# Products with carried state in a retention block: from 128x64 array tiles to eight 64x32 tiles with an exchange of heads in PSUM

## Chip, cores, metric

One core of one Trainium2 chip. The metric is the device time of one execution in microseconds (us), as a median over runs. The kernel before took 1078.23 us (median of 3 runs, 1076.21 to 1079.26).

## The reference

A retention block (a linear attention with a decay per head) feeds an MLP with PReLU; everything is fp32. Cut to what matters:

```python
B, H, S, D = 8, 8, 576, 64
scores = q @ k^T / sqrt(D)                       # per batch and head
Dmat   = gamma[h] ** (i - j) where i >= j else 0
ret    = (scores * Dmat) @ v
x = ret.transpose(0, 2, 1, 3).reshape(B * S, H * D)        # 4608 x 512
h = x @ w_in                                     # 512 -> 2048
out = (max(h, 0) + alpha * min(h, 0)) @ w_out    # 2048 -> 512
```

## The kernel before

TensorE works the matmuls and adds up their results in PSUM, a memory in banks, from which ScalarE and VectorE copy them. Retention is worked in chunks of 64 tokens, nine for a sequence, for two heads at a time: 32 pairs of heads, which the code calls n. Inside a chunk it is scores times v (the "values"). What comes from earlier chunks is q times a carried sum of k^T v (the "products with the sums", one for each of the chunks 1 to 8). Between these small blocks stand units of the MLP, which fill TensorE: 28 records of `ph` and 14 of `po` a unit (a record is one MATMUL entry of the profile).

```python
def half(x):                       # 64 of the 128 partitions
    return slice(x * C, (x + 1) * C)

def states(n, kn, vn):             # k^T v of each chunk, then the carried sums
    ... 32 records of 64x64 matmuls into ps[0], ps[1] ...
    su = attn.tile([P, NJ - 1, D], FP32, tag="su", name=f"su_{n}")   # head h2 in half h2
    ... ScalarE and VectorE form the carried sums in su ...
    for h2 in range(2):            # sm: a 128x128 block diagonal of both heads, zero elsewhere
        nc.scalar.copy(sm[half(h2), :, h2], su[half(h2)])

def values(n, vn, qT, at):
    b, c = pairs[n]
    pv = [ps_tile(n, p2, [P, NM, C], f"pv{p2}_{n}") for p2 in range(2)]   # even, odd chunks
    for m in range(NM):
        for p2 in range(2 if 2 * m + 1 < NJ else 1):
            for h2 in range(2):
                nc.tensor.matmul(pv[p2][half(h2), m], vn[half(p2), m, h2],
                                 at[h2][half(p2), m], start=(m == 0), stop=False, ...)
    for j in range(1, NJ):         # the products with the sums
        for h2 in range(2):
            nc.tensor.matmul(pv[j % 2][half(h2), j // 2], sm[:, j - 1, h2],
                             qT[:, chunk(j)], start=False, stop=(j >= NJ - 2), ...)
    for p2 in range(2):
        put_x(b, c, p2, pv[p2])    # ScalarE copies pv into the MLP's input
```

The product for one head contracts 128 rows, of which 64 are zeros: it uses one half of the array's columns and all its rows, so two such products fit at a time, and half of what they multiply is nothing.

## Time and profile before

| | before |
|---|---|
| median | 1078.23 us |
| span of the profiled run | 1076.6 us |
| TensorE busy | 1054.3 us (98%) |
| a block of products with the sums, from its first start to the next block | 1.082 us, 32 records |
| from the products of pair 8 to the end | 864.08 us |

The prediction below shows the lines and how to read them. One note: the start of this kernel, up to about 200 us, varies from run to run; the last row of the table leaves it out and is the sharper measure. I take it from the timeline, from the start of the first product of pair 8 (212.55 us) to the end of the span:

```profile
212.55 1.15 PE L565 MATMUL pv<-qT,sums 128*64 128x64 f32 x32
```

### The profile page before, as it was taken

Reading aid. Unit: us, or ns where it says so; the run is one execution under the profiler, and the core shown is the slowest. Engines: PE = TensorE matmul, PEld = TensorE weight load, DVE = VectorE, ACT = ScalarE, POOL = GpSimd, SP = SyncE. Lnnn points to the kernel's source line nnn. Section 1 sums busy time; section 2 is a strip of 40 time slices with the busy share of each in tenths; the row PEclk is TensorE's granted clock in tenths of the full one; section 3 lists DMA queues with packets and bytes.
Section 4 is the critical chain, followed back from the end, with each engine's and each line's share of the span. In section 5 each row is a group of like instructions: output and inputs, shape, how many; then the busy total and the mean of one; then the engine's idle time right before and its main releaser. Section 6 shows DMA issues by size and latency. Waiting matters only on the chain.

```text
span 1076.6 us, 25072 instructions
## 1 busy us (share of the span) xinstructions
PE 1054.3 (98%) x10321; PEld 927.9 (86%) x10321; DVE 747.0 (69%) x1958; ACT 191.1 (18%) x549; POOL 217.4 (20%) x260
## 2 busy tenths in 40 slices
PE   6899999999999999999999999999999999999998
PEld 5666666899999999999999999999999999999997
DVE  5688612678687777786777777786768676667575
ACT  3666422211110111110100111111111110000000
POOL 4368743411020102010102110201011000100000
PEclk9989999999999999999999999999999999999999
DMA  8857413212222222211112222122222100000000
GB/s 199 242 155 231 100 25 63 76 36 64 45 65 43 56 46 52 47 43 34 35 43 40 60 46 65 35 65 46 65 46 54 24 21 1 21 1 21 1 21 20
DMA packets 212050, 63.25 MB, mean 59 GB/s; under 512 B 201168, under 2 KB 201184, under 8 KB 211936
## 3 DMA queue, kind: packets, MB, share of 16 engines
q1 hardware_dynamic: 209504, 61.04, 24.2%
q8 instruction: 82, 1.34, 0.5%
q10 hardware_dynamic: 2432, 0.60, 0.3%
q14 instruction: 32, 0.26, 0.1%
HBM read 52.17 MB, written 9.44 MB: 57 GB/s over the span
## 4 chain that ended last, share of the span: by engine, by line
PE 93%; DVE 2%; DMA 2%; ACT 1%; issue 1%; POOL 0%; SPq 0%; ACTq 0%; DVEq 0%
PE ph L392 38%; PE po L314 36%; PE ph L350 5%; PE po L329 4%; PE pv L565 3%; PE pv L560 2%; PE ps L523 2%; PE pu L538 2%; PE pt L494 1%; DMA raw<-in_moe_w_in_dram 1%; DMA w_in<-in_moe_w_in_dram 1%; DVE wc L245 1%; DVE wc L248 0%; DMA a<-in_moe_alpha_dram 0%; DMA kn<-in_k_dram 0%
## 5 line engine op out<-in xcount | busy, mean ns | idle before, releaser
L314 PE MATMUL po<-w_out,g 128*128 128x256 f32 x1792 | 407.8, 379 | 0.0
L314 PEld LDWEIGHTS po<-w_out,g 128*128 128x128 f32 x1792 | 330.8, 190 | 39.7
L403 DVE TENSOR_TENSOR g<-ph,g 128x256 f32<-128x256 f32 (+1 forms) x512 | 187.4, 387 | 180.2 <-PE ph L392 103.6
L392 PE MATMUL ph<-xb,w_in 128*128 128x128 f32 x2048 | 277.7, 279 | 0.0
L392 PEld LDWEIGHTS ph<-xb,w_in 128*128 128x128 f32 x2048 | 253.1, 192 | 8.2 <-issue 0.5
L392 PE MATMUL ph<-xt,w_in 128*128 128x128 f32 x1536 | 213.3, 275 | 0.0
L392 PEld LDWEIGHTS ph<-xt,w_in 128*128 128x128 f32 x1536 | 192.1, 192 | 0.0
L414 DVE TENSOR_TENSOR g<-g 128x128 f32<-128x128 f32 x512 | 144.0, 322 | 7.8
L398 ACT COPY g<-ph 128x128 f32<-128x128 f32 x128 | 34.0, 265 | 479.5 <-PE ph L392 472.0
L462 POOL TENSOR_TENSOR vn<-vn,th 128x512 f32<-128x512 f32 (+1 forms) x60 | 42.0, 718 | 380.9 <-DMA vn<-in_v_dram 380.8
L408 DVE SCALAR_TENSOR_TENSOR g<-g 128x512 f32<-128x512 f32 x128 | 94.3, 737 | 3.9
L406 DVE TENSOR_SCALAR g<-g,alpha 128x256 f32<-128x256 f32 x256 | 88.7, 388 | 4.5
L350 PE MATMUL ph<-xb,w_in 128*128 128x256 f32 x256 | 65.3, 404 | 2.8 <-DVE g L359 2.3
L375 POOL TENSOR_TENSOR xt<-xb,xt 128x256 f32<-128x256 f32 x32 | 25.1, 786 | 175.2 <-ACT xb L451 174.6
L350 PEld LDWEIGHTS ph<-xb,w_in 128*128 128x128 f32 x256 | 48.9, 198 | 13.2 <-issue 4.7
L329 PE MATMUL po<-w_out,g 128*128 128x512 f32 x128 | 57.8, 593 | 1.1 <-DVE g L359 1.1
L451 ACT COPY xb<-pv 128x128 f32<-128x128 f32 (+1 forms) x176 | 29.6, 269 | 129.1 <-PE pv L565 129.1
L329 PEld LDWEIGHTS po<-w_out,g 128*128 128x128 f32 x128 | 24.2, 190 | 24.5 <-issue 22.0
L552 ACT COPY sums<-su 64x512 f32<-64x512 f32 x64 | 39.5, 617 | 29.4 <-DVE su L549 28.6
L527 DVE SCALAR_TENSOR_TENSOR at<-ps,th,mask 128x320 f32<-128x320 f32 x64 | 32.4, 544 | 15.9 <-PE ps L523 15.9
L506 DVE STREAM_TRANSPOSE qT<-qn 128x576 f32<-128x576 f32 x24 | 18.7, 778 | 33.8 <-PE pv L565 30.5
L565 PE MATMUL pv<-qT,sums 128*64 128x64 f32 x1024 | 41.2, 235 | 0.2 <-ACT sums L552 0.2
(90 smaller groups left out, 686.8 us busy)
## 6 DMA issues: line engine op xcount, KB each, us to landing
out_dram<-osb SPq DMA_DIRECT2D x36, 256.0 KB, 2.3
kn<-in_k_dram SPq DMA_DIRECT2D x60, 128.0 KB, 2.9
vn<-in_v_dram SPq DMA_DIRECT2D x60, 128.0 KB, 2.7
kx<-in_k_dram SPq DMA_DIRECT2D x96, 72.0 KB, 2.4
qn<-in_q_dram SPq DMA_DIRECT2D x96, 72.0 KB, 2.5
raw<-in_moe_w_in_dram SPq DMA_DIRECT2D x11, 512.0 KB, 4.3
raw<-in_moe_w_out_dram SPq DMA_DIRECT2D x11, 512.0 KB, 4.6
w_in<-in_moe_w_in_dram SPq DMA_DIRECT2D x5, 512.0 KB, 6.0
```

Source lines behind the costliest of these rows:

```text
L314: nc.tensor.matmul(acc[kb][n // 2][:, n % 2, :], g[:, x, :], w_out[i][:, y, :], start=(i == 0 and n % 2 == 0), stop=(i == NU - 1 and (n % ...
L329: nc.tensor.matmul(acc[kb][m], g[:, 2 * x + m], w_out[i][:, 2 * x:2 * x + 2].rearrange("p x f -> p (x f)"), start=(i == 0 and x == 0), sto ...
L350: nc.tensor.matmul(ph[:, x], w_in[i // UST][:, cc // 2 * 2 + x, cc % 2, f0:f0 + P], xb[kb][:, cc], start=(cc == 0), stop=(cc == NCC - 1))
L392: nc.tensor.matmul(ph[m][:, o], w_in[i // UST][:, l, cc, f0:f0 + P], r[:, cc], start=(n in (0, 3) and cc == 0), stop=(n in (2, 6) and cc = ...
L398: nc.scalar.copy(g[:, 7], ph[0][:, 2])
L403: nc.vector.tensor_tensor(out=o, in0=x0, in1=x1, op=ALU.add)
L406: nc.vector.tensor_scalar(g[:, 4 + 2 * m:6 + 2 * m], g[:, 2 * m:2 * m + 2], 0.0, alpha[:, fc:fc + 1], ALU.min, ALU.mult)
L408: nc.vector.scalar_tensor_tensor(out=g[:, 0:4].rearrange("p x t -> p (x t)"), in0=g[:, 0:4].rearrange("p x t -> p (x t)"), scalar=0.0, in1 ...
L414: nc.vector.tensor_tensor(out=g[:, o, :], in0=g[:, x0, :], in1=g[:, x1, :], op=op)
L462: nc.gpsimd.tensor_tensor(out=t[0:rows, m], in0=t[0:rows, m], in1=th[0:rows, x, None, 2 * c:2 * c + 2, None].to_broadcast([rows, n, 2, D]) ...
L552: nc.scalar.copy(sm[half(h2), :, h2], su[half(h2)])
L565: nc.tensor.matmul(pv[j % 2][half(h2), j // 2], sm[:, j - 1, h2], qT[:, chunk(j)], start=False, stop=(j >= NJ - 2), skip_group_check=True)
```

## The change

Its intent: give each product the 64 rows it needs. A weight tile of 64 rows by 32 columns lets eight matmuls stand in the array (the prediction names the page). Without more, head h2 would always use the rows of half h2 and the columns of half h2, four of the eight tiles. So the odd chunks have their heads exchanged in PSUM (head 0 in partitions 64 to 127), which uses the other four, and the copy out of PSUM puts them back. The block diagonal `sm`, its memset and its two ScalarE copies per pair go away.

```diff
-    sm = const.tile([P, NJ - 1, 2, D], FP32, name="sums")
-    nc.gpsimd.memset(sm, 0.0)
...
             n = min(nm - m, (w - o + 1) // 2)
-            nc.scalar.copy(xb[kb][:, c].rearrange(...)[:, o:o + 2 * n - 1:2], pv[:, m:m + n])
+            to = xb[kb][:, c].rearrange("p (j w) -> p j w", w=C)[:, o:o + 2 * n - 1:2]
+            for h2 in range(2) if par else ():
+                nc.scalar.copy(to[half(h2)], pv[half(1 - h2), m:m + n])
+            if not par:
+                nc.scalar.copy(to, pv[:, m:m + n])
...
-        for h2 in range(2):
-            nc.scalar.copy(sm[half(h2), :, h2], su[half(h2)])
+        return su                                   # su now has bufs=2
...
-                    nc.tensor.matmul(pv[p2][half(h2), m], vn[half(p2), m, h2],
+                    nc.tensor.matmul(pv[p2][half(h2 ^ p2), m], vn[half(p2), m, h2],
...
         for j in range(1, NJ):
             for h2 in range(2):
-                nc.tensor.matmul(pv[j % 2][half(h2), j // 2], sm[:, j - 1, h2],
-                                 qT[:, chunk(j)], start=False, stop=(j >= NJ - 2), ...)
+                for e in range(0, D, 32):
+                    to = (h2 ^ (j % 2)) * D + e
+                    nc.tensor.matmul(pv[j % 2][to:to + 32, j // 2],
+                                     su[half(h2), j - 1, e:e + 32], qT[half(h2), chunk(j)],
+                                     start=False, stop=(j >= NJ - 2), ...)
```

More of the change, by code (lines that the diff above doesn't have):

```diff
@@ L450, in put_x @@
             n = min(nm - m, (w - o + 1) // 2)
-            nc.scalar.copy(xb[kb][:, c].rearrange("p (j w) -> p j w", w=C)[:, o:o + 2 * n - 1:2],
-                           pv[:, m:m + n])
+            to = xb[kb][:, c].rearrange("p (j w) -> p j w", w=C)[:, o:o + 2 * n - 1:2]
[3 more added lines that the diff above has]
+                nc.scalar.copy(to, pv[:, m:m + n])
             m += n
@@ L540, in states @@
                                      skip_group_check=True)
-        su = attn.tile([P, NJ - 1, D], FP32, tag="su", name=f"su_{n}")
+        su = attn.tile([P, NJ - 1, D], FP32, tag="su", bufs=2, name=f"su_{n}")
         g1, g2 = gch[:, 0, c:c + 1], gch[:, 1, c:c + 1]
@@ L550, in states, with values @@
                                        in1=ps[0][:, 1:], op0=ALU.mult, op1=ALU.add)
-        for h2 in range(2):
-            nc.scalar.copy(sm[half(h2), :, h2], su[half(h2)])
-    def values(n, vn, qT, at):
+        return su
+    def values(n, vn, qT, at, su):
         b, c = pairs[n]
@@ L564, in values @@
             for h2 in range(2):
-                nc.tensor.matmul(pv[j % 2][half(h2), j // 2], sm[:, j - 1, h2],
-                                 qT[:, chunk(j)], start=False, stop=(j >= NJ - 2),
-                                 skip_group_check=True)
+                for e in range(0, D, 32):
+                    to = (h2 ^ (j % 2)) * D + e
+                    nc.tensor.matmul(pv[j % 2][to:to + 32, j // 2],
+                                     su[half(h2), j - 1, e:e + 32], qT[half(h2), chunk(j)],
+                                     start=False, stop=(j >= NJ - 2), skip_group_check=True)
         for p2 in range(2):
@@ L595 @@
         load_weights(parts[2])
-        states(n, kn, vn)
+        su = states(n, kn, vn)
         pop_units(cuts[1])
@@ L600 @@
             turned[n + 1] = transposes(n + 1)
-        values(n, vn, qT, at)
+        values(n, vn, qT, at, su)
         del loaded[n]
```

## The prediction

> **What bounds the kernel now.** I read the page's busy rows first, then the table of windows by stage, then the timeline of TensorE around the products that the change touches.
>
> ```profile
> PE 1054.3 (98%) x10321; PEld 927.9 (86%) x10321; DVE 747.0 (69%) x1958; ACT 191.1 (18%) x549; POOL 217.4 (20%) x260
> ```
>
> TensorE is busy for 98% of the span; the next engine, VectorE, for 69%. A share over the whole span can hide stages, so next the windows (columns: stretch, length, then busy time and count of PE, PEld, DVE, ACT, POOL, then granted clock, DMA share, GB/s):
>
> ```profile
> 0.00:60.00 60.00, 45.59 (x619) 36.97 (x620) 38.30 (x97) 32.22 (x77) 28.02 (x42) 0.92 0.87 224
> 60.00:192.00 132.00, 128.53 (x1000) 85.63 (x998) 70.18 (x128) 57.13 (x124) 83.75 (x90) 0.98 0.41 107
> 192.00:915.00 723.00, 723.00 (x7641) 658.00 (x7640) 533.53 (x1430) 92.75 (x316) 97.68 (x119) 1.00 0.22 46
> ```
>
> From 192 to 915 us TensorE has no gap at all: 723.00 of 723.00. The last of the 32 head pairs is worked at 914 us, so there whatever shortens a block of matmuls shortens the kernel by as much, and what leaves ScalarE or GpSimd there is worth nothing. From 60 to 192 us TensorE is idle for only 3.5 us. Only the first 60 us are something else: TensorE has 14 us of idle time, and DMA runs at 87%.
>
> The groups concerned, from the page (busy us, mean ns | idle before, releaser):
>
> ```profile
> L552 ACT COPY sums<-su 64x512 f32<-64x512 f32 x64 | 39.5, 617 | 29.4 <-DVE su L549 28.6
> L565 PE MATMUL pv<-qT,sums 128*64 128x64 f32 x1024 | 41.2, 235 | 0.2 <-ACT sums L552 0.2
> ```
>
> L565 is the product with the carried sums: 16 matmuls per pair, 512 in all, and each fp32 matmul is two records, hence 1024. In all its life it waited 0.2 us for the copies of L552. The mean of 235 ns is a latency, since matmuls overlap, so I take the cost of a block from starts: from its first record to the first record of the next block. Timeline of TensorE in steady state (start us, us, what):
>
> ```profile
> 444.87 0.80 PE L560 MATMUL pv<-at,vn 64*64 64x64 f32 x36
> 445.60 1.15 PE L565 MATMUL pv<-qT,sums 128*64 128x64 f32 x32
> 446.68 1.16 PE L392 MATMUL ph<-xb,w_in 128*128 128x128 f32 x8
> ...
> 459.18 0.81 PE L523 MATMUL ps<-qT,kT 64*64 64x64 f32 x40
> 459.92 1.16 PE L392 MATMUL ph<-xb,w_in 128*128 128x128 f32 x8
> ```
>
> and in another pair:
>
> ```profile
> 906.38 0.69 PE L538 MATMUL pu<-vn,kn 64*64 64x64 f32 x32
> 907.00 1.16 PE L392 MATMUL ph<-xb,w_in 128*128 128x128 f32 x8
> ```
>
> L565 takes 445.60 to 446.68 = 1.08 us for 32 records. L538 does 32 records of the same 64 moving columns in 0.62 us. The difference is the tiling: 128x64 puts two tiles in the array, 64x64 puts four.
>
> **A model from these rows.** Call one record on every tile a round. L538 is 32/4 = 8 rounds in 0.62 us, L523 40/4 = 10 rounds in 0.74, L565 32/2 = 16 rounds in 1.08. From 8 and 16 rounds: (1.08 - 0.62)/8 = 0.0575 us per round, and 0.62 - 8 x 0.0575 = 0.16 us fixed per block. Check: 10 rounds give 0.735, measured 0.74. So a round costs 58 ns with two tiles or four, and a block costs its rounds.
>
> Whether eight fit in a round depends on how fast tiles can be started. Records of L523 that overlap the stretch from 459.00 to the time given, which counts starts (same columns, PE only):
>
> ```profile
> 459.00:459.28 0.28, 0.10 (x4) 1.00 0.00 0
> 459.00:459.29 0.29, 0.11 (x5) 1.00 0.00 0
> 459.00:459.30 0.30, 0.12 (x7) 1.00 0.00 0
> 459.00:459.31 0.31, 0.13 (x8) 1.00 0.00 0
> 459.00:459.34 0.34, 0.16 (x8) 1.00 0.00 0
> 459.00:459.37 0.37, 0.19 (x12) 1.00 0.00 0
> ```
>
> Four starts fall between 459.28 and 459.31: about 7 ns apart, then nothing until the round is over. Eight starts need 8 x 7 = 56 ns, just inside 58. That is the whole margin.
>
> **What the Trainium skill says.** (1) "TensorEngine Tiling (Array Packing)", Available Configurations: 64 rows by 32 columns is 8 tiles; Key Properties: changing the mode drains TensorE. The 0.16 us per block fits that, and the change keeps the number of mode switches in steady state. (2) "TensorE: Matmul & The Clock Gate", Wait - 56ns, not 53.3ns?: starts never come closer than about 25 ns. For tiled matmuls this trace disagrees: 40 in 0.74 us is 18.5 ns each with the fixed part in. (3) The same page, Measured speedup vs the span model: each further tile costs about 4 ns; here I see about 7. (4) "PSUM — Partial Sum Buffer", PSUM bank collisions raise a hardware error: two row tiles must not write one bank and 32-partition quadrant together. With the exchange of heads, odd chunks go to one bank and even ones to the other with the halves swapped, so a quadrant gets one row half in each bank; nothing here shows yet that this runs at full pace.
>
> **The change part by part.**
>
> Matmuls of L565: 16 per pair become 32 (16 x 2 halves of 32 columns), 64 records, on eight tiles: 64/8 = 8 rounds. In the order of the built program, pairs 4 to 31 issue them as four on the odd chunk and four on the even one, eight different tiles in turn. Model: 0.16 + 8 x 0.0575 = 0.62 us, plus four more starts in the last round, 4 x 7 ns = 0.03: 0.65 us. Saved 1.08 - 0.65 = 0.43 us a pair; for the 28 pairs of 4 to 31, all on the TensorE-bound stretch, 28 x 0.43 = **12.0 us**.
>
> Copies of L552: 64 x 617 ns = 39.5 us leave ScalarE (18% busy). Worth nothing after 60 us. The 128x1024 memset of the sums (0.95 us on GpSimd at 1.5 us) goes too; GpSimd then waits for inputs until 6 us, so nothing.
>
> Exchange of heads: the copies of odd chunks into xb become twice as many at half the partitions. 176 copies at about 270 ns now, so some 80 more: +20 us on ScalarE, half of what it gets back. The block before is followed by a 6.3 us unit of the MLP, so the copies stay hidden.
>
> Pairs 0 to 3: the blocks of L565 there run slower (1.9 us, at a clock of 0.92 and mixed with other work), and are 10.4% of the chain of the first 75 us. The order of the built program is poor in two of them: pair 2 issues all even chunks, then all odd ones, so four tiles at a time and no gain; pair 0 is cut by other blocks, some five more mode switches at 0.16 to 0.3 us. Pairs 1 and 3 may save 0.9 us each, and a 0.6 us sums copy at 46 us leaves the chain. I put this at a gain of 1 us, give or take 3.
>
> Sum: 12.0 + 1 = 13. 1078.2 - 13 = **1065.2 us**, 1.2% less.
>
> **The rivals.** (a) Starts bind: a stream of 16 loads and matmuls per 58 ns, twice what L523 needs, may not be fed. At 10 ns a start the block is 64 x 10 + 160 = 0.80 us, saving 0.28 x 28 = 8: about 1070. At 13 ns a start it is 0.99 and the time some 1075. Against it: the 7 ns seen inside a round. For it: that was four in a row, never eight. (b) The two row halves take turns at a bank, since for the first time both write one bank at once (the tiling page warns that different row tiles cannot): four tiles at a time, 16 rounds, 1.08 us, and the time stays at 1077 to 1079. Against it: disjoint quadrants. (c) The 25 ns floor of the skill holds for 32-column tiles: 64 x 25 + 160 = 1.76 us, +0.68 x 28 = 19 us more, 1097. The 18.5 ns above speaks against it. (d) VectorE becomes the bound: it is 74% busy in the steady stretch (533.53 of 723), and 1.5% less span does not fill it. (e) The removed waits on ScalarE free the start more than I think: the first 60 us hold 14 us of idle TensorE, but DMA at 87% is the more likely limit; at most 5 us, 1060.
>
> **Range and chances.** I give the full eight tiles about 70%, a feed limit (a) 20%, (b) 6%, (c) 3%. With the start's give or take 3 us: 1060 to 1073. Faster by over 2% means below 1056.7, or 21.5 us; all of L565 from pair 4 on is 28 x 1.08 = 30 us, so the block would have to fall to 0.35 us or the start give much: 4%. Slower by over 2% needs (c): 3%.
>
> **What would show it.** Right: in steady state the block that replaces L565 has 64 records and 0.62 to 0.70 us from its first start to the next block; windows still show TensorE without a gap from about 192 us; 28 pairs account for about 12 us. Wrong: a block of 0.8 us and more with starts evenly 10 ns or more apart (a); rounds of four (b); a gap before the next block, or a stretch from 192 us on with TensorE idle, waiting for xb; or a start that moves by more than 3 us.

## The result, and the profile after

The changed kernel took 1071.45 us (median of 4 runs, 1071.20 to 1071.68) against 1077.85 for the kernel before (4 runs): 6.4 us less. The ratio of the two is 0.9941, with a 95% interval of 0.9924 to 0.9958. Ratios here are the mean time of one kernel's fast runs over that of the other's fast runs of the same rounds, so not quite the ratio of the medians quoted.

The page of the changed kernel, and its windows by stage (columns as before):

```profile
PE 1048.6 (98%) x11345; PEld 919.7 (86%) x11345; DVE 750.2 (70%) x1958; ACT 178.1 (17%) x565; POOL 216.4 (20%) x259
```

```profile
192.00:915.00 723.00, 723.00 (x8483) 656.95 (x8474) 541.89 (x1437) 84.25 (x335) 103.22 (x125) 1.00 0.22 47
```

TensorE still has no gap in the long stretch. Nothing took the place of the removed work there: whatever the change gained in a block, it kept. The timeline of the block, beside which the prediction's lines at 445.60 and 446.68 are to be read:

```profile
443.65 0.86 PE L567 MATMUL pv<-qT,su 64*32 64x64 f32 x64
444.43 1.16 PE L387 MATMUL ph<-xb,w_in 128*128 128x128 f32 x8
```

The block has 64 records and takes 0.788 us from first start to next block, to within 1 ns in all 28 pairs from 4 to 31; the printed starts, rounded, give 0.78. It was 1.082, and I had predicted 0.65. So each pair saves 0.294 us, not 0.43. Why is to be seen in the counts of the block's records that overlap the stretch from 443 to the time given:

```profile
443.00:443.69 0.69, 0.04 (x7) 1.00 0.00 0
443.00:443.72 0.72, 0.07 (x8) 1.00 0.00 0
443.00:443.89 0.89, 0.24 (x32) 1.00 0.00 0
443.00:443.96 0.96, 0.31 (x33) 1.00 0.00 0
443.00:444.15 1.15, 0.50 (x51) 1.00 0.00 0
443.00:444.30 1.30, 0.65 (x64) 1.00 0.00 0
```

Up to the 32nd record all goes as predicted: eight starts in under 50 ns, then a wait for the round to end, and four rounds, 32 records, in 0.24 us. Then one single start in 70 ns, and the other 31 records take until 444.29. The starts themselves show it more finely: rounds at 0, 80, 136 and 192 ns after the first start, the 32nd record at 239 ns, the 33rd at 267, the 34th at 323, and from 331 ns on a step every 16.8 ns, in which two records start, or only one (at first and at the end). From 331 to 642 ns, the last start, that is 10.7 ns a record.

The same measure as in the table above:

```profile
212.95 0.86 PE L567 MATMUL pv<-qT,su 64*32 64x64 f32 x64
```

From the products of pair 8 (212.95 us) to the end (1069.96) are 857.01 us, against 864.08. The difference of 7.07 is 24 x 0.294. The rest of the result lies in the start, where the changed kernel reached the products of pair 8 0.40 us *later*, though pairs 4 to 7 had saved 4 x 0.294 = 1.18 us. Where that went is in the chain of work that ended last (start, length, what). Before:

```profile
98.26 5.99 DMA w_in<-in_moe_w_in_dram
...
107.58 5.38 PE ph L350 x16
```

and after:

```profile
97.79 6.83 DMA w_in<-in_moe_w_in_dram
...
107.92 6.31 PE ph L345 x16
```

A piece of w_in lands at 104.25 us before and at 104.62 after; ScalarE and VectorE then work off a chain, and only then may TensorE go on. In this run the piece took longer, TensorE waited 3.5 us in place of 2.3, and its 16 records after the wait took 6.31 us in place of 5.38, with the granted clock lower (0.72 in the windows from 104 to 116.3 us, against 0.86 before). So in this pair of profiles, what was gained before 104 us was lost to a DMA's landing and to the lower clock. The clock is of this one profile: in the other two of the changed kernel (e7, e11), and in both of the kernel before, the 16 records took 5.38 us. The longer wait is not: it is 3.2 to 4.4 us in all three profiles of the changed kernel, 1.9 and 2.3 in the two of the kernel before (before, e9).

### The profile page after: what moved, and what is told of

The parts are those of the page before. It is cut to its first block, busy times and chain, and to the rows that moved or that the text cites. A ratio compares the mean times of both kernels' runs of the same rounds, so it can differ in the third digit from the quotient of the medians.

```text
span 1070.0 us, 27161 instructions
## 1 busy us (share of the span) xinstructions
PE 1048.6 (98%) x11345; PEld 919.7 (86%) x11345; DVE 750.2 (70%) x1958; ACT 178.1 (17%) x565; POOL 216.4 (20%) x259
## 4 chain that ended last, share of the span: by engine, by line
PE 94%; DVE 2%; DMA 1%; issue 1%; ACT 1%; SPq 0%; POOL 0%; ACTq 0%; DVEq 0%; POOLq 0%
PE ph L387 39%; PE po L309 36%; PE ph L345 5%; PE po L324 4%; PE pv L567 3%; PE pv L560 3%; PE ps L521 2%; PE pu L536 2%; PE pt L492 1%; DMA w_in<-in_moe_w_in_dram 1%; DVE wc L240 0%; DVE wc L243 0%; DMA raw<-in_moe_w_in_dram 0%; DMA a<-in_moe_alpha_dram 0%; DVE w_in L245 0%
## 5 line engine op out<-in xcount | busy, mean ns | idle before, releaser
L401 DVE TENSOR_SCALAR g<-g,alpha 128x256 f32<-128x256 f32 x256 | 93.3, 406 | 4.5
L448 ACT COPY xb<-pv 64x128 f32<-64x128 f32 (+1 forms) x160 | 38.1, 238 | 158.9 <-PE pv L567 157.0
L370 POOL TENSOR_TENSOR xt<-xb,xt 128x256 f32<-128x256 f32 x32 | 25.2, 788 | 171.8 <-ACT xb L450 171.2
L354 DVE SCALAR_TENSOR_TENSOR g<-g,nalpha,ph 128x256 f32<-128x256 f32 x32 | 13.9, 477 | 39.8 <-ACT ph L350 39.8
L541 ACT COPY su<-pu 128x256 f32<-128x256 f32 x32 | 11.9, 371 | 135.3 <-PE pu L536 135.3
```

Source lines behind the costliest of these rows:

```text
L401: nc.vector.tensor_scalar(g[:, 4 + 2 * m:6 + 2 * m], g[:, 2 * m:2 * m + 2], 0.0, alpha[:, fc:fc + 1], ALU.min, ALU.mult)
L448: nc.scalar.copy(to[half(h2)], pv[half(1 - h2), m:m + n])
```

## The experiments

Two theories of the block of 0.79 us. **Feed and queue**: the first 32 records (64 instructions, a load and a matmul each) stand ready and start at 7 ns each; those behind them are delivered more slowly, whatever the array could take. **Eight tiles**: eight tiles of 32 columns do not overlap fully, because both row halves write one PSUM bank at once or for another reason in the array, which costs each round some 20 ns ((0.788 - 0.16)/8 = 0.078 us in place of 0.058).

### e1: the change without the exchange of heads

```diff
-                    to = (h2 ^ (j % 2)) * D + e
+                    to = h2 * D + e
```

and `half(h2)` for the values, whole copies in put_x.

> The change without the exchange of heads: 64 rows by 32 columns as in the changed kernel, but odd chunks keep their heads in place, so that only four of the eight tiles are used; the sums copies stay away, and the odd chunks need no split copies. Theory F (feed: the block of 0.79 us comes from the rate at which TensorE's sequencer delivers instructions once those waiting in its queue are used up, about 8.4 ns for a load and a matmul): four tiles need a record only every 14.5 ns, so rounds of 58 ns rule again and the block of 64 records takes 0.16 + 16 x 0.0575 = 1.08 us, as before the change. The copies taken off ScalarE are then shown to be worth nothing: 1075 to 1079 us. Rival B (eight tiles do not overlap fully in the array or at PSUM, because both row halves write one bank): row halves write disjoint partitions of a bank here too, so the rounds would be about 78 ns and the block 1.4 us, and the time 1087 us.

```profile
407.86 1.10 PE L567 MATMUL pv<-qT,su 64*32 64x64 f32 x64
408.88 1.16 PE L387 MATMUL ph<-xb,w_in 128*128 128x128 f32 x8
```

The block took 1.028 us, near the 1.08 of the feed theory and far from 1.4. The same 64 records on the same kind of tile run with no pause: starts come in fours, after a first round of 80 ns every 56 ns to the end. So 16 rounds of 56 ns with 32-column tiles, a little less than the 58 ns with 64 columns. The time was 1077.23 us (4 runs, 1074.16 to 1081.05), ratio 1.0014 (0.998 to 1.0048): as before the change. From the products of pair 8 to the end it took 862.76 us, 1.32 less than before, and 24 x (1.082 - 1.028) = 1.30. So the sums copies that left ScalarE (39.5 us of its busy time) are worth nothing on that stretch, as predicted. Of the change's 7.07 us there, 1.32 come with the 64x32 form even when only four of its tiles are used, and the other 5.75 with the use of all eight.

### e2: twice the columns on the eight tiles (wrong result)

```diff
+                    m, x = min(j // 2, NM - 2), min(j, NJ - 2) * C
-                    nc.tensor.matmul(pv[j % 2][to:to + 32, j // 2],
-                                     su[half(h2), j - 1, e:e + 32], qT[half(h2), chunk(j)],
+                    nc.tensor.matmul(pv[j % 2][to:to + 32, m:m + 2],
+                                     su[half(h2), j - 1, e:e + 32], qT[half(h2), x:x + 2 * C],
```

> The changed kernel with each of its 32 products moving 128 columns instead of 64 (wrong result on purpose): the same count of instructions on the same eight tiles, twice the columns. A round of 128 columns is 111.5 ns (28 records of the MLP product in 3.12 us), so a record is needed only every 14 ns. F: the feed keeps up, and the block takes 0.16 + 8 x 0.1115 + 0.03 = 1.08 us, 0.29 more than with 64 columns instead of 0.43 more. B, with a loss that grows with the columns (78 ns in place of 58): 0.16 + 8 x 0.150 + 0.03 = 1.39 us; with a fixed loss of 20 ns in each round: 1.24 us.

```profile
408.69 1.16 PE L568 MATMUL pv<-qT,su 64*32 64x128 f32 x64
409.77 1.16 PE L387 MATMUL ph<-xb,w_in 128*128 128x128 f32 x8
```

The block took 1.086 us, against 1.08 for the feed and 1.24 or 1.39 for the eight tiles. Twice the work on the same tiles costs only 0.30 us more, because the rounds are now long enough for the feed. The starts show the slower feed here too: the first eight fall within 46 ns, but those from the 41st to the 48th take 98 ns, and the round still lasts 109 ns, as the rounds ahead of it do:

```profile
408.00:409.25 1.25, 0.56 (x40) 1.00 0.00 0
408.00:409.36 1.36, 0.68 (x48) 1.00 0.00 0
```

Both row halves write one bank all the time here, so this also removes the bank as a cause.

### e3: the products issued twice (wrong result)

```diff
-        for j in range(1, NJ):
+        for j in [*range(1, NJ), *range(1, NJ)]:
```

> The changed kernel with its 32 products issued twice in a row (wrong result on purpose): 128 records in one block in place of 64. F: the second 64 records all come at the rate of the feed, 8.4 ns each: 0.79 + 0.54 = 1.33 us. If the loss were a single pause behind the first 32 records, and 58 ns for eight tiles after that: 0.79 + 8 x 0.058 = 1.25 us. B, 78 ns in each round: 0.79 + 8 x 0.078 = 1.42 us; a pause that comes again behind every 32 records: about 1.43 us.

Most blocks took 1.415 us. Five from pair 4 on took 1.8 to 3.7; in the longest, TensorE stood still for 2 us inside the block, and the profile shows nothing that it waited for ("issue"):

```profile
583.69 1.45 PE L567 MATMUL pv<-qT,su 64*32 64x64 f32 x124
587.18 0.30 PE L567 MATMUL pv<-qT,su 64*32 64x64 f32 x4 [2.04 <-issue]
```

That fits a feed that runs dry, but what held it up is not shown. I had put the feed theory at 1.33, with 8.4 ns for each record after the 32nd; that missed. The count of starts says what is right (the first start is at 424.40):

```profile
424.00:424.66 0.66, 0.26 (x32) 1.00 0.00 0
424.00:424.98 0.98, 0.58 (x59) 1.00 0.00 0
424.00:425.31 1.31, 0.91 (x94) 1.00 0.00 0
424.00:425.64 1.64, 1.24 (x126) 1.00 0.05 15
```

After the first 32 records in 0.24 us, some 32 come in each 0.33 us: 10.3 ns a record. Within such a stretch two records come every 16.8 ns (8.4 a record), with a slower passage about every 32 records: the last case of the expectation, 1.43 us. The figure 1.42 of the other theory fits as well here, but e1, e2 and e8 exclude it.

### e8: half of the products (wrong result)

```diff
-        for j in range(1, NJ):
+        for j in (1, 2, 7, 8):
```

> The changed kernel with half of its products (chunks 1, 2, 7 and 8 alone; wrong result on purpose): 32 records in the block on the eight tiles, as many as start without a loss in the changed kernel. Q (the loss comes only behind the 32nd record): four full rounds of 56 ns and no pause, 0.24 us to the last start and 0.15 to the next block: 0.39 us. Rival (each round of eight tiles loses 20 ns): 0.16 + 4 x 0.0785 + 0.03 = 0.50 us. The stretch from pair 8's product to the end: 857.0 - 24 x 0.40 = 847.4 us for Q, 850.1 for the rival.

```profile
403.64 0.45 PE L567 MATMUL pv<-qT,su 64*32 64x64 f32 x32
404.02 1.16 PE L387 MATMUL ph<-xb,w_in 128*128 128x128 f32 x8
```

The block took 0.384 us (0.39 expected of the feed and queue, 0.50 of the other), and the stretch from pair 8's product to the end 847.32 us (847.4 expected). So a block of 32 records on eight tiles is free of loss, and the whole loss of the changed kernel's block, 0.788 - 2 x 0.384 + 0.15 (one fixed part counted twice) = 0.17 us, stands behind its 32nd record.

### e5: the same cover of the array with half the records

With the exchange of heads, 64x64 tiles would cover the array too: four tiles, 32 records. But then the values and the products have the same tiling, and different row halves would write the same partitions of a bank with nothing to order them. A small copy out of `pv` on ScalarE, which the products must wait for, orders them. The MLP units of a pair are now dealt to four places instead of three.

```diff
+        if n >= 8 and between:
+            seen = attn.tile([P, 2], FP32, tag="seen", name=f"seen_{n}")
+            for p2 in range(2):
+                nc.scalar.copy(seen[:, p2:p2 + 1], pv[p2][:, 0, 0:1])
+            pop_units(between)                      # an MLP unit
+        w = D if n >= 8 and between else 32
...
-                for e in range(0, D, 32):
+                for e in range(0, D, w):
```

> From pair 8 on the products take 64 rows and 64 columns, with the exchange of heads: 32 records on four tiles, which cover the array as the eight do, with half the instructions. A unit of the MLP stands between values and products (with a small copy out of PSUM on ScalarE that orders the two), since both blocks now have the same tiling and different row halves would write the same partitions of a bank. F: the block takes what the states block takes for 32 records on four tiles, 0.62 us; saved against the changed kernel 24 x (0.79 - 0.62) = 4 us: about 1067.5 us. B (row halves sharing a bank cost the time): the block stays at 0.79 us, and the time at 1071 to 1072 us.

```profile
814.59 0.80 PE L560 MATMUL pv<-at,vn 64*64 64x64 f32 x36
815.31 1.16 PE L387 MATMUL ph<-xb,w_in 128*128 128x128 f32 x8
...
821.66 0.69 PE L573 MATMUL pv<-qT,su 64*64 64x64 f32 x32
822.28 1.16 PE L387 MATMUL ph<-xb,w_in 128*128 128x128 f32 x8
```

The block took 0.625 us, as the feed theory had it. The time did not follow: 1071.7 us (6 runs) where about 1067.5 was expected, ratio 0.9944 (0.992 to 0.9968), and the stretch from pair 8's product to the end took 857.65 us where 857.01 - 24 x 0.163 = 853.1 was due. TensorE had no gap. The missing 4.55 us, 0.19 a pair, are the price of one more visit to small tiles, which is paid in the neighbours. The timeline of the kernel before, between the lines at 446.68 and 459.18 that the prediction shows, has it:

```profile
449.91 3.19 PE L314 MATMUL po<-w_out,g 128*128 128x256 f32 x14
452.94 1.05 PE L392 MATMUL ph<-xb,w_in 128*128 128x128 f32 x8
456.06 3.19 PE L314 MATMUL po<-w_out,g 128*128 128x256 f32 x14
```

The first product of a unit takes 449.91 - 446.68 = 3.23 us behind a small block, and 456.06 - 452.94 = 3.12 behind another unit. The second takes 452.94 - 449.91 = 3.03 ahead of a unit, and 459.18 - 456.06 = 3.12 ahead of a small block. Together 0.20 us, over and above the 0.16 us inside the small block. The unit that e5 puts between its two small blocks shows the same: 821.66 - 815.31 = 6.35 us, against 3.12 + 3.03 = 6.15 for one between units.

### e6: the four-tile products in two halves of 32 moving columns

```diff
+                    for x in (0, 32) if w == D else ():
+                        nc.tensor.matmul(pv[j % 2][to:to + w, j // 2, x:x + 32],
+                                         su[half(h2), j - 1, e:e + w],
+                                         qT[half(h2), j * C + x:j * C + x + 32], ...)
```

> The four-tile form with an MLP unit between values and products, but from pair 8 on each product is issued in two halves of 32 moving columns: again 64 records in the block, on four tiles of 64 columns. Theory Q (feed and queue: 32 records, each a load and a matmul, start at 7 ns, and those behind them come with pauses at about 10 ns): the block is slower than its columns need, about 0.75 to 0.85 us, like the eight-tile block. Rival (the loss belongs to eight tiles of 32 columns): rounds of some 29 ns for four tiles, 16 of them: 0.16 + 16 x 0.029 + 0.02 = 0.64 us. The kernel's time should be 1070 to 1076 us.

The block took 1.126 us, more than either had said, and the one run 1081.94 us: a failed experiment for its question. Four records still came in each 58 ns although they moved half the columns, so something other than the moving columns sets the round. The Trainium skill, "TensorE: Matmul & The Clock Gate", LDWEIGHTS, puts the ns of a load at its columns over 1.2, which gives an estimate of 53 ns for 64 columns and would fit; no run here takes it apart. With rounds that long, the feed was not what bound.

### e4: the changed form from pair 4 on only

Pairs 0 to 3 keep the block diagonal, its copies and the order of before.

```diff
+                if n < 4:
+                    nc.tensor.matmul(pv[j % 2][half(h2), j // 2], sm[:, j - 1, h2], qT[:, chunk(j)], ...)
-                for e in range(0, D, 32):
+                for e in range(0, D, 32) if n >= 4 else ():
```

> The changed form from pair 4 on only; pairs 0 to 3 are worked as before the change, in the order of before, with its sums copies. If the changed order of the start is what costs the changed kernel some 1.6 us there (28 pairs at 0.294 us are 8.2, its span fell by 6.6), this kernel runs at about 1069.8 us. If the start only varies by chance (a DMA's landing and TensorE's clock), it runs at the changed kernel's time, 1071.5 us within 1, and its stretch from pair 8's product to the end is the changed kernel's 857 us.

1069.73 us (6 runs, 1067.23 to 1072.50), ratio 0.9945 (0.9921 to 0.997). By itself this is the figure that had been expected if the changed order of the start costs 1.6 us; but it has to be held against the changed kernel on the same chip, which is e7.

### e7, e9 and e11: the two kernels again

No edit.

> The changed kernel once more, for its time beside the others on this chip and for how much its start varies. Steady stretch from pair 8's product to the end: 857 us again, within 0.2. Time of pair 8's product: somewhere between 209 and 214 us; if the start varies by chance it moves by over 1 us against the first profile's 212.95.

> The kernel before once more, for its profile alone: the stretch from pair 8's product to the end should be 864.1 us again within 0.2, and the time of pair 8's product should move by over 1 us against 212.55 if the start varies by chance.

> The changed kernel beside it on the same chip: 1069 to 1072 us, its stretch from pair 8's product to the end 857.0 us.

e7 took 1069.79 us (6 runs, 1069.09 to 1071.95), ratio 0.9948 (0.9924 to 0.9971), on the chip of e4; e11 1071.29 us (6 runs), ratio 0.9949 (0.9925 to 0.9974), on another. Between e4 and e7 no difference shows (medians 1069.73 and 1069.79, means 1069.8 and 1070.0), so nothing says that the form of the first four pairs costs the start. But e4's runs fall in two groups, 1067.23 to 1068.22 and 1071.24 to 1072.50, and its median in the gap between them, so six runs are a weak test. What the start does by itself:

| profile | first product of pair 8, us | from there to the end, us |
|---|---|---|
| before | 212.55 | 864.08 |
| before again (e9) | 213.68 | 864.07 |
| after | 212.95 | 857.01 |
| after again (e7) | 211.21 | 857.01 |
| after beside (e11) | 212.48 | 857.02 |
| late only (e4) | 208.50 | 857.01 |
| no exchange (e1) | 209.70 | 862.76 |

The right column repeats to 0.01 us, the left one moves by up to 1.7 us for the same kernel. The kernel before also ran in two clusters on the later chips, from 1072.25 to 1074.71 and from 1076.26 to 1079.29 us. In the first comparison all four of its runs fell in the upper one, as both its profiles do; over all 37 fast runs of it, and 16 of the changed kernel, the means are 1076.4 and 1070.8, 5.7 us apart, so the 6.4 us quoted first are rather high. With that spread the start's share of the change (predicted as a gain of 1 us, seen as a loss of 1.6 in the first two profiles) is not resolved. The order of the first four pairs is not shown to matter, and e4 cannot exclude an effect of some 2 us; e4's profile, the earliest at pair 8, is of the quickest of its six runs.

### e10: half the products on four tiles, half on eight

The experiments name three things: 32 records on eight tiles are free, four 64x64 tiles need half the records, and a further visit to small tiles costs 0.2 us. The conflict in e5 came from the products whose row half differs from that of the values in their bank. If the heads are exchanged by the chunk's place in PSUM (m odd) instead of by its parity, half of the products (row half equal to the values' one) can follow the values in the same 64x64 tiling, with no drain and no conflict: 16 records. The other half takes 64x32 on all eight tiles: 32 records.

```diff
-        for j in range(1, NJ):
-            for h2 in range(2):
-                for e in range(0, D, 32):
-                    to = (h2 ^ (j % 2)) * D + e
+        for same in (True, False):
+            w = D if same else 32
+            for j in range(1, NJ):
+                h2 = j % 2 if same else 1 - j % 2
+                for e in range(0, D, w):
+                    to = (h2 ^ (j // 2 % 2)) * D + e
```

with `half(h2 ^ (m % 2))` for the values, and copies out of PSUM chunk by chunk, 13 a pair instead of 8.

> A version meant to beat both, built on what the runs before showed: only the first 32 records of an eight-tile block are free of loss, a four-tile block of 64 columns needs half the records, and an extra visit to small tiles costs some 0.2 us. The heads are exchanged by the chunk's place in PSUM (every second one) instead of by the chunk's parity. Then half of the products, those whose row half is that of the values of their bank, follow the values in the same 64x64 tiling without a drain: 16 records on four tiles, 4 rounds. The other half takes 64x32 on all eight tiles: 32 records, 4 rounds, no pause. Q: values and products together, from the first start of the values to the next block, are 0.73 + 4 x 0.0575 + 0.384 = 1.34 us, against 0.73 + 0.79 = 1.52 in the changed kernel; the stretch from pair 8's product to the end falls by 23 to 24 times 0.17, from 857.0 to about 853 us; the time is 1065.5 us, 4.5 less than the changed kernel. Rival: the 13 copies out of PSUM per pair in place of 8 hold up ScalarE's other copies, and TensorE waits: gaps after pair 8, and a time of 1070 us or more.

The timeline of values and products, to be held against 728 + 788 ns for the changed kernel (the third row merges both tilings):

```profile
820.26 0.74 PE L562 MATMUL pv<-at,vn 64*64 64x64 f32 x34
...
820.86 0.82 PE L571 MATMUL pv<-qT,su 64*64 64x64 f32 x46
821.61 0.60 PE L387 MATMUL ph<-xb,w_in 128*128 128x128 f32 x3
```

821.61 - 820.26 = 1.35 us, against 1.52 (1.34 expected). TensorE has no gap from 192 us on. From the first values of pair 8 to the end e10 took 853.66 us and the changed kernel 857.74: 4.08 less, which is 24 x 0.17. Its time was 1069.37 us (6 runs, 1067.57 to 1070.66), ratio 0.9935 (0.991 to 0.996), beside 1071.29 for the changed kernel on the same chip. The gain on the steady stretch is sure; of the whole time only some 2 us show, where 4.5 had been expected. In its profile the start came later by 1 us or so (it reached the values of pair 8 at 213.11, the changed kernel at 212.22 and 211.75); with the spread of the start one profile can't say whether that is its own. The waits hint that it is: up to 60 us, MLP products waited three times, 1.7 us in all, for ScalarE's copies into xb, which those of the changed kernel did in none of its three profiles. So the expectation's rival, copies that hold TensorE up, may have come true in the start, though not after pair 8. e10 is the fastest of the correct versions on the steady stretch; the intervals of the ratios overlap.

## Why the prediction was right or wrong

Predicted 1065.2 us, 13 less; measured 1071.45, 6.4 less. The direction was right, and so was the mechanism up to the 32nd record of a block; the size was half of what I said. That the time lies inside the range is the range's width, which took in rival (a) at 1070, and not the eight tiles at full pace on which the 1065.2 rests.

**TensorE as the bound, gain kept block by block: right.** 7.07 us of the stretch from pair 8 on are 24 times what one block lost.

**Removed sums copies worth nothing, split copies about 20 us more on ScalarE: right.** e1 leaves 0.02 us for the copies; the copies into xb went from 39.3 us (25.2 + 14.1) to 59.2 (24.9 + 13.2 + 14.0 + 7.1), all behind the next unit.

**Rounds: the model held, and the failed step is the one after it.** "64/8 = 8 rounds" at 0.0575 us "plus four more starts in the last round ... 0.65 us" assumed that 64 records can be fed at 7 ns each because four in a row had been. The first 32 were, eight to a round (e8: 0.384 us a block). The next 32 came at about 11 ns each with a pause ahead of them. That is the feed limit of rival (a), which I gave 20% and for which I had written 0.80 us at 10 ns a start; it measured 0.788. That the figures agree so well is luck: rival (a) had even starts from the first record on, and neither that nor "0.8 us and more", its sign, was seen. As a term of the sum: the block's saving was put at 28 x 0.43 = 12.0 us and was 28 x 0.294 = 8.2 us. I had seen the margin, 56 ns of starts in a round of 58, and still asked only how fast four records start, not how long such a pace can last.

**The other rivals: excluded.** (b): both row halves write one bank at full pace (e2, e8). (c): starts 7 ns apart are far below 25. (d): VectorE is busy for 541.89 of the 723.00 us, and TensorE has no gap. (e): no profile of the changed kernel has a start that is 5 us shorter.

**The start: not resolved.** I had said a gain of 1 us, give or take 3. The first two profiles show a loss of 1.6, of which a later landing of one weight piece and the lower clock after that wait make up the visible part; other profiles of the same kernels differ by as much. The wait for that piece is longer in all three profiles of the changed kernel: TensorE comes to that point some 1 to 3 us earlier there, and the piece is not yet there.

What stays open: whether the depth of the queue (64 instructions by the page that the last section names, which are 32 records) or the rate at which instructions reach it sets the pace behind the 32nd record. The pause, in which the 33rd record starts close to the end of the first (at 267 ns; the first lasts 240), speaks for the first; the even step of 16.8 ns after it speaks for the second. No run here separates the two.

## What to carry to other kernels

Cutting a matmul into smaller tiles multiplies the instructions: before counting on n tiles at a time, ask whether a block has more load-and-matmul pairs than stand ready in the queue (32 here), and prefer the largest tile that still covers the array. A visit to another tiling also costs the blocks beside it, so count visits, not only rounds. And when the start of a kernel scatters by more than the gain, measure from a fixed block in the steady part to the end: here that repeats to 0.01 us.

## What the Trainium skill lacked or had wrong

- "TensorE: Matmul & The Clock Gate", Wait - 56ns, not 53.3ns?: starts are said never to come closer than about 25 ns, without the limit to one tile that the page's own 4 ns (next point) implies. On separate tiles eight start within 50 ns, about 7 ns apart (after).
- The same page, Measured speedup vs the span model: about 4 ns for each further tile; here about 7 ns (before, after).
- The same page gives the queue a depth of 64, but not what that means for packed tiles: 32 records (64 instructions) run at the pace of the tiles (e8), and those behind them at about 10.3 ns each (e3: some 32 records in each 0.33 us), which is slower than the 7 ns a record (eight in 56 ns) that eight tiles of 64 moving fp32 columns can take.
- "TensorEngine Tiling (Array Packing)", Key Properties: a change of mode drains TensorE, without a figure. Here a block of small tiles has a fixed part of 0.16 us, and the 128x128 blocks beside it lose another 0.20 us (e5).
- The same page, Gotcha 1, says that different row tiles cannot access one PSUM bank at the same time. With disjoint 32-partition quadrants they did so at full pace and with the right result (after; e8 for the pace); "PSUM — Partial Sum Buffer", PSUM bank collisions raise a hardware error, which quotes the same rule, also has the measured one, per bank and quadrant, and that fits.
- No page gives the round of packed fp32 tiles as such: 58 ns for 64 moving columns with 64-column weights (before), 56 ns with 32-column weights (e1), 109 ns for 128 columns with 32-column weights (e2).
